# Moving weight conversions earlier and writing out the instruction order of 45 units by hand, in a kernel of attention and two MLP blocks

## The chip, the core and the metric

The kernel runs on one core of a Trainium2 chip. The metric is the device time of one execution in microseconds (us). The core has five engines that work side by side, each with its own queue in order: TensorE (PE in the profile, with its weight loads as PEld), VectorE (DVE), ScalarE (ACT), GpSimd (POOL), and SyncE (SP), which here issues nearly every DMA. An engine takes its instructions in the order in which the compiled program lists them; an instruction that waits holds up all that stand behind it on that engine.

## The reference

Inputs are float32. Batch is 4, sequence 576, width 512 (8 heads of 64).

```python
x = attention(q, k, v)                      # local band + pooled, (4, 576, 512)
xn = (x - mean) / sqrt(var + 1e-6) * g_ln
x = x + relu(xn @ w_ch1) @ w_ch2            # first MLP, hidden width 2048
h = relu(x.T @ w_tok1) @ w_tok2             # token mixing over the sequence, 576 -> 256 -> 576
u = x + h.T
out = u + relu(u @ w_ch1') @ w_ch2'         # second MLP, hidden width 1536
```

The weights arrive as float64 words (two int32 each), so the kernel must turn them into float32 on the chip and then split each into a high and a low float32r part; every product is three matmuls (high by high, high by low, low by high).

## The kernel before, in words

**Units.** The 2304 tokens are 18 tiles of 128, taken two at a time as 9 chunks of 256. A unit is one chunk against one block of 128 hidden columns: `g1` (12 matmuls, L883) into a PSUM bank of pool `h`, `relu` on ACT (L897), `low` on DVE (L901), then `g2` (6 matmuls, L916) into the chunk's accumulators `acc`. The first MLP has 16 blocks, so units 0 to 143 are chunks 0 to 8; the second has 12, so units 144 to 251 are chunks 9 to 17. `base[c]` is the first unit of chunk c: `base[7]` is 112, `base[8]` 128, `base[9]` 144, `base[10]` 156. From unit 157 on, units 1 to 10 of a chunk are done in pairs (`g1_pair` L994, `pair_sums`, `g2_pair` L1033) with fewer matmuls. A unit's program order is g1 of the next unit, its relu, its low, the steps of list `mid`, g2 of this unit, and the steps of list `bg`; the function `put(position, step)` files a step in the `mid` (whole number) or `bg` (half) list of a unit. A chunk's end (`evac` L925, `store`) writes the sums back.

**Weights.** A piece is half a block's weights, 128 x 512 values, 512 KB as it arrives. `convert_steps` makes float32 of it with three DVE instructions (L261, L266, L271) from a staging buffer `st` into a buffer `cv`, then splits it (ACT L276, DVE L279). For the second MLP the resident weight buffers come free only while chunk 8 runs, so 20 pieces (blocks 1 to 10) are converted ahead in `pre_f32` (L1331) and written by a DMA to a scratch tensor `w_scr` (L1339, 256 KB); `b_load` (L1341) reads a block back into `st` (L1347, 512 KB) and `b_split` (L1349) splits it (ACT L1358, DVE L1361). The four pieces of blocks 0 and 11 are never written out: they are loaded (L1325) and converted where they are split. There are three `st` buffers and, in this part, two `cv` buffers. `load_tok` (L1061) loads and converts the nine pieces of the token weights.

**Other steps around it.** A chunk's input is centred (`ln_center`), transposed in 32 x 32 blocks on DVE (`xt_t` L814), put in place by 4 groups of 4 DMAs for each of its 2 tiles (`xt_dma` L822), and split (`xp_hi` ACT L834, `xp_lo` DVE L839). Token mixing loads a tile (`xs_load` L1096), splits it on ACT (L1100) and POOL (L1101), and multiplies (`tok1` L1115, `tok2` L1150). `tq_load` and `tq_sums` (L977, L985, L986) make the combined weights for the pairs, from `w_scr`.

**Order.** Units 0 to 111 follow a table of steps written out by hand (`STEPS`), emitted under `manual_schedule`, which keeps the written order on every engine. What comes after is placed by a scheduler that works on a modelled timeline: it may put a step earlier than the program lists it, between the table's steps too. Only some instructions are held at their place in the program by `keep_in_program_order`: the first DVE instruction of each `pre_f32`, the first ACT instruction of each `b_split`, the first of each `ln_rstd` and of each `tq_sums`.

**Steps that the change and the prediction touch.** At `bt` = 112: `close_att` (L1300), all nine `load_tok`, and the first two `pre_load`. At units 113 to 132 (L1366): one `pre_f32` each. From unit 130 (`bw` = 128): `b_load` and, at half units from 131, `b_split` (L1369 to L1372). `put_prep1` (L1166) files a first-MLP chunk's preparation and `put_prep2` (L1181) that of a second-MLP chunk, with all eight groups of `xt_dma` directly behind the transposes; `put_tok` (L1174) files a batch's token mixing.

Of the kernel before, what the change touches and what calls it, by code (L numbers as in the profile page):

```python
# [9 lines left out]
I32 = mybir.dt.int32  # L10
# [34 lines left out]
FAST = 11  # L45
QF = DM // 2
# [22 lines left out]
    1; xt_lo 0 0; s_max 4; s_exp 4; ln_center 0 1; av_pe 3 1 acc; load 4 vw; raw 2 1; av_norm 3 1; s_pe 5 g; xt_pe 0
    1 acc; s_max 5; xt_hi 0 1; s_exp 5; load 5 vw; xt_lo 0 1; ex_pe 3 1 acc; t_pe 4 1 acc; x_add 3 1; c_a 4; load 6  # L70
    qk; ln_center 1 0; g1 0; ln_center 1 1; t_copy 4 1; td_pe 5 0 g; relu 0; c_b 4; t_pe 4 0 acc; td_copy 5 0; td_pe
    5 1 g; t_copy 4 0; raw 3 0; td_copy 5 1; xt_pe 1 0 acc; xt_hi 1 0; xt_lo 1 0; t_pe 5 1 g; avd_pe 5 g; load 6 vg;
    xt_pe 1 1 acc; t_copy 5 1; v_sums 4; xt_hi 1 1; avd_norm 5; low 0; t_pe 5 0 g; xt_lo 1 1; c_c 4; avd_pe 4 acc;
    t_copy 5 0; c_hi 4; c_lo 3; up_write 5; av_pe 4 g; av_z 4; g1 1; avd_norm 4; c_a 5; raw 3 1; av_act 4; relu 1;
    g1 2; c_lo 4; c_b 5; c_a 6; g2 0; low 1; av_pe 5 g; g2 1; g1 3; relu 2; c_c 5; av_z 5; low 2; g2 2; c_hi 5; c_b
    6; up_write 4; c_lo 5; c_c 6; av_act 5; up_read 5; c_a 7; relu 3; raw 4 0; low 3; load 6 vw; s_pe 6 g; c_hi 6;
    g1 4; g2 3; c_b 7; g1 5; c_lo 6; raw 4 1; c_c 7; c_hi 7; s_max 6; relu 4; s_exp 6; relu 5; loc_write 5; t_pe 6 0
    g; q_sums 6; c_a 8; c_lo 7; t_copy 6 0; low 4; c_b 8; c_a 9; c_c 8; g2 4; raw 5 0; d_pe 6 g; c_b 9; low 5; raw 5
    1; c_hi 8; c_c 9; c_hi 9; g1 6; raw 6 0; c_lo 8; d_max 6; g2 5; d_exp 6; c_a 10; c_lo 9; g1 7; load 7 qk; c_b
    10; relu 6; relu 7; td_pe 6 1 g; low 6; td_copy 6 1; c_c 10; c_a 11; low 7; td_pe 6 0 g; g2 6; v_sums 6; c_b 11;  # L80
    t_pe 6 1 g; raw 6 1; td_copy 6 0; c_hi 10; t_copy 6 1; avd_pe 6 g; c_lo 10; g2 7; c_c 11; c_a 12; avd_norm 6; g1
    8; g1 9; c_hi 11; relu 8; load 7 vg; c_b 12; c_lo 11; raw 7 0; c_c 12; c_a 13; low 8; q_sums 7; c_hi 12; av_pe 6
    g; c_b 13; c_lo 12; raw 7 1; g2 8; relu 9; c_c 13; low 9; c_hi 13; av_z 6; c_a 14; c_lo 13; g1 10; loc_read 5;
    av_act 6; c_b 14; relu 10; g2 9; c_a 15; g1 11; c_c 14; c_b 15; low 10; c_hi 14; c_c 15; s_pe 7 g; relu 11; c_hi
    15; raw 8 0; c_lo 14; s_max 7; c_a 16; s_exp 7; loc_write 4; low 11; c_b 16; g2 10; raw 8 1; g1 12; g2 11; c_lo
    15; c_c 16; relu 12; up_write 6; c_a 17; low 12; c_b 17; raw 9 0; raw 9 1; c_hi 16; d_pe 7 g; loc_write 6; g1
    13; d_max 7; c_lo 16; g2 12; g1 14; relu 13; c_c 17; d_exp 7; c_a 18; low 13; c_hi 17; relu 14; t_pe 7 0 g; c_b
    18; td_pe 7 1 g; t_copy 7 0; g2 13; c_lo 17; v_sums 7; raw 10 0; c_c 18; c_a 19; up_read 4; c_hi 18; low 14;
    loc_read 4; td_pe 7 0 g; g1 15; relu 15; g2 14; g1 16; av_add 5; raw 10 1; td_copy 7 1; c_b 19; c_lo 18; c_c 19;
    td_copy 7 0; low 15; raw 11 0; c_a 20; av_add 4; load 7 vw; c_hi 19; t_pe 7 1 g; c_b 20; c_lo 19; g2 15; c_c 20;  # L90
    g1 17; relu 16; c_hi 20; low 16; rstd; raw 11 1; relu 17; low 17; t_copy 7 1; g2 16; g1 18; relu 18; avd_pe 7 g;
    c_a 21; c_lo 20; c_b 21; g2 17; c_a 22; loc_read 6; g1 19; low 18; c_c 21; up_read 6; raw 12 0; g2 18; c_b 22;
# [12 lines left out]
    v_red 12 0; d_max 8; d_exp 8; v_mul 12 1; g2 31; relu 32; td_pe 8 1 g; td_copy 8 1; evac 29 1; v_red 12 1; td_pe
    8 0 g; evac 31 0; low 32; td_copy 8 0; load 9 qk; g1 33; v_mul 12 2; avd_pe 8 k; evac 29 0; relu 33; v_red 12 2;
    evac 31 1; av_pe 8 g; xt_dma 3 0 1; store 29 1; avd_norm 8; g1 34; v_mul 12 3; low 33; av_z 8; g2 32; v_red 12
    3; av_act 8; xt_dma 3 0 2; store 31 0; q_sums 9; s_pe 9 k; d_pe 9 g; store 29 0; v_mul 12 4; relu 34; rstd 2;
    v_red 12 4; g2 33; v_mul 12 5; load 9 vg; xt_dma 3 0 3; low 34; load 9 vw; xp_hi 3 0; s_max 9; loc_write 8; g1
    35; s_exp 9; load 10 qk; v_red 12 5; d_max 9; relu 35; g2 34; d_exp 9; g1 36; v_mul 12 6; xt_t 3 1; relu 36;  # L110
    t_pe 9 0 k; v_sums 9; v_red 12 6; t_copy 9 0; low 35; td_pe 9 0 k; s_pe 10 g; v_soft1 12; td_copy 9 0; up_write
    8; td_pe 9 1 k; t_pe 9 1 k; low 36; s_max 10; g2 35; v_sexp 12; td_copy 9 1; v_soft2 12; t_copy 9 1; avd_pe 9 k;
    g1 37; v_gm 12 0; store 31 1; avd_norm 9; s_exp 10; relu 37; q_sums 10; v_gm 12 1; loc_read 8; av_pe 9 g; low
    37; d_pe 10 k; xt_dma 3 1 0; g1 38; g2 36; g1 39; v_ga 12 1; v_load 13; up_read 8; av_z 9; av_add 8; xt_dma 3 1
# [85 lines left out]
def block_kernel(ctx: ExitStack, tc: tile.TileContext, qk, vw, vh, vg, g_ln, wa, t1, t2, wb, band, near, lv, edge, out):  # L200
# [46 lines left out]
    wt = {}  # L247

    wa, wb, t1, t2 = (w.bitcast(I32) for w in (wa, wb, t1, t2))

    def stage(n):
        return sp["pool"].tile([128, 2 * QW], I32, tag="st", name="st", bufs=sp["n"])[:, :2 * n]

# [57 lines left out]
    def split_unit(i, part, pinned=True):  # L311
        first, *rest = split_steps(i, part)
        ins = first()
        if pinned:
            tc.keep_in_program_order(ins)
# [1211 lines left out]
```

## Time and profile before

| | before |
|---|---|
| median of 3 runs | 886.04 us (884.27 to 886.44) |
| the profiled execution's own time | 888.04 us |
| its span, first to last instruction | 886.2 us |
| PE busy | 857.1 us (97%) |
| PEld busy | 775.9 us (88%) |
| DVE busy | 604.6 us (68%) |
| ACT busy | 302.0 us (34%) |
| POOL busy | 211.0 us (24%) |
| mean granted TensorE clock | 0.996 |

How to read it: busy time is the time in which at least one instruction of an engine is running. The profiled execution is one of its own; 1.84 us of it lie outside the span. A row's number after the start is its duration; a bracket at its end is the idle time just before it on its engine and what ended that. "SPq" rows are DMAs being issued, not their transfers.

### The profile page before, as it was taken

To read this page: it belongs to the slowest core of one execution; us is meant where nothing else is said; L and a number is where in the kernel's file an instruction comes from. 1 tells how busy PE (TensorE), PEld (TensorE's weight loads), DVE (VectorE), ACT (ScalarE), POOL (GpSimd) and SP (SyncE) were. 2 spreads that over 40 slices of the span, in tenths; PEclk is the share of its full clock that TensorE was granted. 3 is DMA by queue.
4 is the path that set the end of the run, shared out by engine and by line. 5 is a ranking of instruction groups with operands and counts; after the bars stand their busy time and mean duration, and the time that the engine had idled before them with its cause. 6 is when DMAs were issued, how large, how long until landed. Compare 5 with 4: busy or idle time off the path is not lost.

```text
span 886.2 us, 18074 instructions
## 1 busy us (share of the span) xinstructions
PE 857.1 (97%) x6778; PEld 775.9 (88%) x6778; DVE 604.6 (68%) x1345; ACT 302.0 (34%) x829; POOL 211.0 (24%) x213
## 2 busy tenths in 40 slices
PE   7989999999999999999997999999999999999997
PEld 6878899888889999888997887889999998999997
DVE  5999989998988776832376856665546545455454
ACT  5665535354321111312111134343333242323332
POOL 7731233467873510101000001001021011000000
PEclk9999999999999999999999999999999999999999
DMA  8646776467662522542187748322132122112100
GB/s 282 191 147 227 225 238 198 148 197 222 168 156 70 138 50 60 157 120 65 38 240 264 244 138 239 99 91 64 39 83 71 42 68 62 23 40 57 23 26 24
DMA packets 132518, 111.56 MB, mean 126 GB/s; under 512 B 79384, under 2 KB 105016, under 8 KB 132432
## 3 DMA queue, kind: packets, MB, share of 16 engines
q1 hardware_dynamic: 132432, 110.42, 43.5%
q8 instruction: 53, 0.87, 0.4%
q14 instruction: 33, 0.27, 0.1%
HBM read 80.73 MB, written 21.77 MB: 116 GB/s over the span
## 4 chain that ended last, share of the span: by engine, by line
PE 60%; DVE 17%; DMA 11%; SPq 6%; issue 3%; POOL 2%; ACT 1%; DVEq 0%; ACTq 0%; POOLq 0%
PE h L883 15%; PE acc L916 13%; PE h L994 11%; PE g L1033 6%; SPq L822 5%; PE acc L1033 4%; PE k L916 2%; DMA w_scr<-cv 2%; PE k L1115 2%; PE k L1150 2%; DMA et<-loc_scr 1%; DVE cv L266 1%; DMA st<-w_scr 1%; DVE ht L901 1%; DMA st<-in_wb_dram 1%
## 5 line engine op out<-in xcount | busy, mean ns | idle before, releaser
L883 PEld LDWEIGHTS h<-xt,w 128*128 128x128 f32 x2064 | 267.9, 191 | 19.0 <-DVE ht L901 5.6
L883 PE MATMUL h<-xt,w 128*128 128x256 f32 x2064 | 277.4, 284 | 5.6 <-DVE ht L901 5.0
L916 PE MATMUL acc<-w,ht 128*128 128x512 f32 x840 | 221.1, 398 | 4.5 <-DVE ht L901 3.9
L916 PEld LDWEIGHTS acc<-w,ht 128*128 128x128 f32 x840 | 150.0, 190 | 36.6 <-DVE ht L901 6.9
L897 ACT ACTIVATE ht<-h 128x256 fp32r<-128x256 f32 x156 | 60.0, 385 | 231.9 <-PE h L883 167.6
L994 PE MATMUL h<-xt,w 128*128 128x256 f32 x960 | 123.1, 283 | 0.0
L994 PEld LDWEIGHTS h<-xt,w 128*128 128x128 f32 x960 | 119.4, 191 | 2.7 <-issue 1.0
L901 DVE SCALAR_TENSOR_TENSOR ht<-h,ht 128x256 fp32r<-128x256 f32 x156 | 65.0, 417 | 63.8 <-ACT ht L897 63.0
L1101 POOL TENSOR_TENSOR xs<-xs 128x512 fp32r<-128x512 f32 x20 | 26.4, 1330 | 336.0 <-ACT xs L1100 229.2
L1011 DVE TENSOR_TENSOR hf<-hf 128x128 f32<-128x128 f32 x160 | 42.2, 304 | 65.3 <-ACT hf L1005 64.0
L1015 DVE TENSOR_TENSOR h<-hf,h 128x512 fp32r<-128x512 f32 x80 | 48.5, 643 | 22.8 <-ACT h L1014 22.7
L1014 ACT ACTIVATE h<-hf 128x512 fp32r<-128x512 f32 x80 | 42.1, 570 | 39.1 <-DVE hf L1011 39.1
L1005 ACT ACTIVATE hf<-h 128x256 f32<-128x256 f32 x80 | 26.3, 381 | 81.4 <-PE h L994 78.7
L688 POOL TENSOR_TENSOR lp<-lqk 128x576 f32<-128x576 f32 x28 | 40.0, 1428 | 42.7 <-DVE ls L694 30.6
L1048 POOL TENSOR_TENSOR x<-x,xc 128x512 f32<-128x512 f32 x8 | 11.3, 1413 | 159.8 <-ACT xc L1045 159.8
L659 POOL TENSOR_TENSOR x<-x,et 128x256 f32<-128x256 f32 (+2 forms) x40 | 33.0, 848 | 47.7 <-DMA et<-loc_scr 37.8
L271 DVE SCALAR_TENSOR_TENSOR cv<-st,cv 128x512 int32<-128x512 int32 (+4 forms) x63 | 43.1, 687 | 0.6
L839 DVE TENSOR_TENSOR xt<-xt 128x512 fp32r<-128x512 f32 x30 | 21.7, 724 | 31.6 <-ACT xt L834 30.4
L266 DVE SCALAR_TENSOR_TENSOR cv<-st,cv 128x512 int32<-128x512 int32 (+4 forms) x63 | 42.4, 675 | 0.6
L1033 PE MATMUL g<-w,h 128*128 128x256 f32 x240 | 40.7, 279 | 0.0
L261 DVE TENSOR_SCALAR cv<-st 128x512 int32<-128x512 int32 (+4 forms) x63 | 27.3, 434 | 16.1 <-DMA w_scr<-cv 10.5
L834 ACT ACTIVATE xt<-xt 128x512 fp32r<-128x512 f32 x30 | 18.9, 631 | 54.9 <-DMA xt<-xc 51.5
(245 smaller groups left out, 1234.1 us busy)
## 6 DMA issues: line engine op xcount, KB each, us to landing
st<-in_wa_dram SPq DMA_DIRECT2D x28, 512.0 KB
st<-in_wb_dram SPq DMA_DIRECT2D x24, 512.0 KB
xt<-xc SPq DMA_DIRECT2D x480, 16.0 KB
qk<-in_qk_dram SPq DMA_DIRECT2D x13, 581.0 KB
w_scr<-cv SPq DMA_DIRECT2D x20, 256.0 KB
st<-w_scr SPq DMA_DIRECT2D x10, 512.0 KB
x_scr<-x SPq DMA_DIRECT2D x18, 256.0 KB
x<-x_scr SPq DMA_DIRECT2D x9, 512.0 KB
```

What stands on the lines that cost most here:

```text
L266: nc.vector.scalar_tensor_tensor(out=f, in0=h, scalar=-0x40000000, in1=f, op0=ALU.bitwise_and, op1=ALU.bitwise_or)
L271: nc.vector.scalar_tensor_tensor(out=f, in0=l, scalar=29, in1=f, op0=ALU.logical_shift_right, op1=ALU.bitwise_or)
L822: nc.sync.dma_start(out=f32(xT[c])[32 * q:32 * q + 32, :, 1, n:n + 32], in_=xts[c, j][32 * i:32 * i + 32, :, q, :])
L883: nc.tensor.matmul(out=hp[:, :CN], lhsT=w[:, 0, a, kk * 128:(kk + 1) * 128], rhs=xT[c][:, kk, e, :], start=(n == 0), stop=(n == 3 * KD - 1),)
L897: nc.scalar.activation(out=t[:, 0], in_=hps[i][:, :CN], func=ACTF.Relu)
L901: nc.vector.scalar_tensor_tensor(out=t[:, 1], in0=hp[:, :CN], scalar=0.0, in1=f32(t[:, 0]), op0=ALU.max, op1=ALU.subtract)
L916: nc.tensor.matmul(out=acc[c, j], lhsT=t[:, a, j * 128:(j + 1) * 128], rhs=w[:, 1, e, :], start=(m == 0 and n == 0), stop=(last and n == 2),)
L994: nc.tensor.matmul(out=hp[:, k], lhsT=w[:, 0, a, kk * 128:(kk + 1) * 128], rhs=xT[c][:, kk, e, :], start=(n == 0), stop=(n == 3 * KD - 1),)
L1011: nc.vector.tensor_tensor(out=f[:, o], in0=f[:, x], in1=f[:, y], op=op)
L1014: nc.scalar.activation(out=hi, in_=v, func=ACTF.Copy)
L1015: nc.vector.tensor_tensor(out=lo, in0=v, in1=f32(hi), op=ALU.subtract)
L1033: nc.tensor.matmul(out=acc[c, k] if first else acc[c, k][:, o], lhsT=t[:, a, a_], rhs=tq["z"][k - 2] if first else w[:, e], start=first, s ...
```

## The change

The nine token pieces and the first seven of the pieces for scratch are converted by steps in the table; the other eleven follow in units 114 to 126. The steps are split: for scratch into load (`pl`), conversion (`pc`) and write (`pw`), for token pieces into load (`tl`), conversion with the high part (`tc`) and low part (`td`). There are three `cv` buffers instead of two. Six pieces are converted where they are split: both of block 0 and the first halves of blocks 1, 4, 7 and 11 (before, the four of blocks 0 and 11); the other 18 go through scratch (before, 20). Units 112 to 156 are emitted under `manual_schedule`; from unit 157 on, the scheduler places the steps as before. Transposes' DMAs are filed group by group, and token mixing of batches 0 and 1 is filed two units earlier.

The steps put into the table, each after the step named:

```
low 86:   close; tl 0; tl 1; tl 2        low 100:  td 8; pl 2; pc 0
low 90:   tc 0; tc 1                     low 103:  pw 0; pl 3; pc 1
low 91:   td 0; td 1; tl 3; tl 4; tc 2; tc 3
low 92:   td 2; td 3; tl 5; tl 6; tc 4   low 104:  pw 1; pl 4; pc 2
low 94:   td 4; tl 7; tc 5               low 105:  pw 2; pl 5; pc 3
low 95:   td 5; tl 8; tc 6               low 106:  pw 3; pl 6; pc 4
low 97:   td 6; pl 0; tc 7               low 107:  pw 4; pl 7; pc 5
low 99:   td 7; pl 1; tc 8               low 109:  pw 5; pl 8; pc 6
low 110:  rstd 7
```

```diff
+W1D = (1, 4, 7, 11)
...
     def put_prep1(c, e):
         for j in range(CT):
-            if c > 2:
-                put(e - 9.5 + j, ln_center, c, j)
-                put(e - 8.5 + j, xt_turn, c, j, None)
-                put(e - 3 + j, xt_part, c, j)
-        put(e + 4, ln_rstd, c)
+            put(e - 14.5 + 3 * j, ln_center, c, j)
+            put(e - 14 + 3 * j, lambda c=c, j=j: xt_t(c, j))
+            for i in range(4):
+                put(e - 13.5 + 4 * j + i, xt_dma, c, j, i)
+            put(e - 7.5 + 5 * j, xp_hi, c, j)
+            put(e - 7 + 5 * j, xp_lo, c, j)
+        put(e + 1.5, ln_rstd, c)
...
-            put(u + n, xs_load, b, n)
+            put(u + n if n > 1 else u + n - (1.5 if b else 3), xs_load, b, n)
...
-            put(e - 10 + 0.5 * j, lambda c=c, j=j: xt_turn(c, j, uch[c][:, j]))
-            put(e - 3 + j, xt_part, c, j)
+            put(e - 10 + 0.5 * j, lambda c=c, j=j: xt_t(c, j, uch[c][:, j]))
+            for i in range(4):
+                put(e - 9.5 + 3 * j + 0.75 * i, xt_dma, c, j, i)
+            put(e - 5 + 3 * j, xp_hi, c, j)
+            put(e - 4.5 + 3 * j, xp_lo, c, j)
...
+    pre = [(m, part) for m in range(1, UB) for part in range(NPC) if part or m not in W1D]
-    pre = [(m, part) for m in range(1, FAST) for part in range(NPC)]
...
-        sp["n"], sp["cv"] = 3, 2
+        sp["n"], sp["cv"] = 3, 3
...
-    put_tok(0, base[NCH - 1] - 4)
-    put_tok(1, base[NCH - 1] + 3)
+    put_tok(0, base[NCH - 1] - 6)
+    put_tok(1, base[NCH - 1] + 1)
+    def direct(m, part):
+        return m == 0 or part == 0 and m in W1D
     def b_load(m):
...
+            if direct(m, part):
+                b_raw(m, part)
+            elif direct(m, 0):
+                f = sp["pool"].tile([128, QW], I32, tag="cv", name="cv", bufs=sp["cv"])
+                ld_w["f", m, part] = f.bitcast(F32)
+                nc.sync.dma_start(out=f.bitcast(F32), in_=w_scr[m][:, part * QW:])
+            elif part == 0:
+                t = stage(QW).bitcast(F32)
+                nc.sync.dma_start(out=t, in_=w_scr[m])
...
-    for k in range(len(pre)):
-        put(bt + 1 + k, pre_load, k + 2)
-        put(bt + 1 + k, pre_f32, k)
-    put(bw + 2, b_load, 0)
+    for k, u in zip(range(7, len(pre)), (2, 3, 5, 6, 8, 9, 10, 11, 12, 13, 14)):
+        put(bt + u, pre_write, k - 1)
+        put(bt + u, pre_load, k + 2)
+        put(bt + u, pre_f32, k)
+    put(bt + 15, pre_write, len(pre) - 1)
     for m in range(UB):
-        put(bw + 3 + m, b_load, m + 1)
-        put(bw + 3.5 + m, b_split, m)
+        put(bw + 1 + m, b_load, m)
+        put(bw + 3 + m, b_split, m)
+        put(bw + 3.5 + m, b_lo, m, 0)
+        put(bw + 4 + m, b_lo, m, 1)
     for c in range(NCH, 2 * NCH):
-        put_prep2(c, base[c] - 1)
+        put_prep2(c, base[c] - (3 if c == NCH else 1))
...
+    with tc.manual_schedule():
+        walk(UNITS, 157)
+    man[0] = False
+    walk(157, NSEQ)
```

`b_split` now emits the conversion and the ACT high part, and `b_lo` the low part (and, for a direct piece, both parts of the split). `walk(lo, hi)` is the loop over units that stood at the end before.

## Rows read from the trace of the kernel before

**Rows 1.** The page's second part: busy tenths in 40 slices of 22 us.
```profile
PE   7989999999999999999997999999999999999997
```

**Rows 2.** Windows: length, busy time (count) of PE, PEld, DVE, ACT, POOL, clock, DMA share, GB/s.
```profile
400.00:433.00 33.00, 33.00 (x200) 28.19 (x199) 6.22 (x13) 6.41 (x15) 3.88 (x3) 1.00 0.15 43
433.40:485.60 52.20, 47.18 (x304) 42.72 (x302) 33.85 (x75) 7.58 (x19) 0.00 (x0) 0.98 0.72 226
485.60:589.70 104.10, 100.51 (x576) 86.64 (x577) 70.39 (x150) 34.44 (x76) 3.96 (x3) 0.98 0.56 168
480.00:485.00 5.00, 0.54 (x5) 0.34 (x3) 0.95 (x2) 0.38 (x1) 0.00 (x0) 0.83 0.59 217
485.00:490.00 5.00, 4.44 (x17) 4.06 (x18) 5.00 (x11) 0.00 (x0) 0.00 (x0) 0.50 0.61 172
```

**Rows 3.** PE's waits from 433 to 590: who waited for what, us in total, times, longest.
```profile
PE h L883 <- DVE ht L901: 5.0, 1, 5.0
PE acc L916 <- DVE ht L901: 1.8, 2, 1.4
PE k L1115 <- ACT xs L1100: 1.1, 1, 1.1
PE acc L916 <- ACT ht L897: 0.5, 1, 0.5
```

**Rows 4.** Timeline around the long wait: start, us, engine, line, operation.
```profile
478.94 0.69 DVE L271 SCALAR_TENSOR_TENSOR cv<-st,cv 128x512 int32<-128x512 int32 x1
...
480.58 0.38 ACT L897 ACTIVATE ht<-h 128x256 fp32r<-128x256 f32 x1 [2.43 <-PE h L883]
484.01 0.43 DVE L261 TENSOR_SCALAR cv<-st 128x512 int32<-128x512 int32 x1 [4.38 <-DMA w_scr<-cv]
...
485.08 0.42 DVE L901 SCALAR_TENSOR_TENSOR ht<-h,ht 128x256 fp32r<-128x256 f32 x1
```

**Rows 5.** The chain that ended last, in order of time: start, us, what.
```profile
425.54 1.43 PE h L883 x12
426.97 2.75 PE acc L916 x12
...
477.37 6.55 DMA w_scr<-cv
...
485.56 2.93 PE h L883 x12
488.49 3.56 PE acc L916 x12
...
532.22 6.39 DMA st<-w_scr
```

**Rows 6.** DVE's groups from 433 to 600: busy us, mean ns, idle before and releaser.
```profile
L271 DVE SCALAR_TENSOR_TENSOR cv<-st,cv 128x512 int32<-128x512 int32 x24 | 17.5, 733 | 0.4
L266 DVE SCALAR_TENSOR_TENSOR cv<-st,cv 128x512 int32<-128x512 int32 x24 | 16.3, 686 | 0.4
L1361 DVE TENSOR_TENSOR w<-st,w 128x512 fp32r<-128x512 f32 x20 | 13.2, 698 | 10.4 <-ACT w L1358 10.4
L261 DVE TENSOR_SCALAR cv<-st 128x512 int32<-128x512 int32 x24 | 10.1, 425 | 15.3 <-DMA w_scr<-cv 10.5 <-DMA st<-in_wb_dram 4.9
```

**Rows 7.** Timelines of SP, and of PE, POOL and DVE, in four places.
```profile
508.76 1.54 PE L1115 MATMUL k<-xs,t1w 128*128 128x512 f32 x6
...
516.15 13.63 SPq L822 DMA_DIRECT2D xt<-xc  x20
...
598.09 1.02 DVE L1011 TENSOR_TENSOR hf<-hf 128x128 f32<-128x128 f32 x4 [0.79 <-ACT hf L1005]
...
617.21 2.56 POOL L1101 TENSOR_TENSOR xs<-xs 128x512 fp32r<-128x512 f32 x2 [77.52 <-PE h L883]
617.71 2.61 DVE L1011 TENSOR_TENSOR hf<-hf 128x128 f32<-128x128 f32 x4 [0.73 <-ACT hf L1005]
...
620.90 0.50 PE L1033 MATMUL g<-tg,h 128*128 128x256 f32 x2 [1.44 <-ACT h L1014]
```

More of the change, by code (lines that the diff above doesn't have):

```diff
@@ L111 @@
[L111 to L114, printed above, removed]
-    1; v_gm 12 2; av_act 9; load 10 vg; xt_dma 3 1 2; d_max 10; v_ga 12 2; t_pe 10 1 g; v_gm 12 3; d_exp 10; relu
@@ new lines, in block_kernel @@
+    sp2_ctx = ExitStack()
+    steps = {f.__name__: f for f in (
+        q_sums, v_sums, s_max, s_exp, d_max, d_exp, t_pe, t_copy, td_pe, td_copy, avd_pe, avd_norm, ex_pe, x_add, expand,
+        up_write, up_read, loc_write, av_norm, av_act, load, fill, consts, band_in, masks, ln_center, xt_pe, xt_hi, xt_lo, g1,
+        relu, low, g2, evac, store, s_pe, d_pe, vec_open, v_load, v_loadv, v_mul, v_red, v_soft1, v_sexp, v_soft2, v_gm,
+        v_ga, v_store, loc_read, xt_t, xt_dma, xp_hi, xp_lo,
+    )}
@@ new lines, in block_kernel, with emit @@
+    steps.update(
+        close=close_att, tl=tok_load, tc=tok_conv, td=tok_lo, pl=pre_load, pc=pre_f32, pw=pre_write, av_pe=av_any, av_add=add_run, raw=load_unit, rstd=lambda c="first": ln_rstd(c, False), av_z=lambda n: av_norm(n, 0),
+        **{name: conv_step(k) for k, name in enumerate(("c_a", "c_b", "c_c", "c_hi", "c_lo"))},
+    )
+    def emit(table):
+        for step in table.split(";"):
+            name, *args = step.split()
+            steps[name](*(int(a) if a.isdigit() else a for a in args))
@@ new lines, in block_kernel @@
+    with tc.manual_schedule():
+        for z in rz:
+            nc.vector.memset(z, 1.0)
+        make_identity(nc, ident)
+        nc.vector.tensor_copy(identr, ident)
+        emit(STEPS)
+    rota[:] = ["g", "k"]
+    nl[0] = nsp[0] = len(pieces)
+    for c in range(8, NCH):
+        put_prep1(c, base[c] - 1)
+    bt = base[NCH - 2]
+    put(base[NCH - 1] - 5, rota.__setitem__, slice(None), ["g"])
+    put_tok(0, base[NCH - 1] - 6)
+    put_tok(1, base[NCH - 1] + 1)
+    def direct(m, part):
+        return m == 0 or part == 0 and m in W1D
@@ L1341, in b_load @@
     def b_load(m):
-        if m in (0, FAST):
-            for part in range(NPC):
+        t = None
+        for part in range(NPC):
+            if direct(m, part):
                 b_raw(m, part)
-        elif m < FAST:
-            t = ld_w["f", m] = stage(QW).bitcast(F32)
-            nc.sync.dma_start(out=t, in_=w_scr[m])
+            elif direct(m, 0):
+                f = sp["pool"].tile([128, QW], I32, tag="cv", name="cv", bufs=sp["cv"])
+                ld_w["f", m, part] = f.bitcast(F32)
[3 more added lines that the diff above has]
+                nc.sync.dma_start(out=t, in_=w_scr[m])
+            if t is not None:
+                ld_w["f", m, part] = t[:, part * QW:(part + 1) * QW]
```

390 lines of the change are left out of this document (198 added, 192 removed).

## The prediction

> **What bounds the kernel now.** The page's second part comes first: PE is busy in nearly every slice [rows 1]. Its 857.1 us of 886.2 leave 29.1 us idle, so only time in which PE idles or runs slowly can be won. Windows tell where. In 400 to 433, while the table's last units run, PE has no gap, while DVE is busy for 6.2 of 33 us [rows 2]. In 433.4 to 485.6 (units 112 to 127, where the pieces are converted for scratch) PE idles 52.20 - 47.18 = 5.0 us; in 485.6 to 589.7 (units 128 to 156, the blocks read back and split, token mixing) 104.10 - 100.51 = 3.6 us [rows 2]. PE's waits name the releasers: one wait of 5.0 us of a g1 for `low`, 1.8 us in two waits of g2 for `low`, 1.1 us for the ACT split of a token tile, 0.5 us for a relu [rows 3].
>
> The timeline shows how the 5.0 us arise [rows 4]. DVE ends a conversion at about 479.6; its next one, at 484.01, sat idle 4.38 us until a write `w_scr<-cv` had landed, since with two `cv` buffers piece k waits for the write of piece k-2. `low` stands behind it on DVE: its relu began at 480.58, it itself only at 485.08, and the PSUM bank that the next g1 needs is freed by it. The chain gives that write 6.55 us from issue to landing [rows 5]. The wait costs once more after it: the granted clock falls to 0.83 and 0.50 of full in the two windows of 5 us [rows 2], the lower level (1.2 GHz), and the next 12 g1 matmuls take 2.93 us and the 12 of g2 3.56 us, where the chain has 1.43 and 2.75 us before [rows 5]: 1.50 + 0.81 = 2.3 us.
>
> **The yardstick.** A unit is 1.43 + 1.38 = 2.81 us of PE. relu and low take 0.38 + 0.42 us [rows 4], some 0.9 us with the steps between, and their result is needed only after one g2 and one g1: `low` may be late by 2.81 - 0.9 = 1.9 us before PE stops. A token-mixing step of 6 matmuls adds about one g2, 1.4 us, judged by its like-shaped matmuls [rows 5, 7].
>
> **The change part by part.**
>
> *Earlier conversions.* One piece is 0.43 + 0.69 + 0.73 = 1.84 us of DVE [rows 6]. Seven move into units 100 to 109. With `low` at 0.42 that is 2.3 us in a unit of 2.8 us. Beside DVE's 6.2 us in 33 they fit, also with the token pieces, which merely spread over more units. Cost nothing; the cover is PE's own work, and if a load is late `low` has its 1.9 us. Left for units 114 to 126 are 11 pieces in 13 units, where 20 were to be done in 20 units with the transposes and splits between.
>
> *Third `cv` buffer and separate writes.* A write is issued in the step after its conversion, so SP no longer waits for DVE in front of it. Piece k now waits for the write of k-3, filed two units (5.6 us) before it. A write as slow as the worst row, 6.55 us, would be late by 0.9 us, less than the 1.9 us of slack. So the 5.0 us and the 2.3 us of slow clock go: 7.3 us. That is a size from one wait seen whole, and both ends are near: if a rest of the wait stays, it is below the limit and costs nothing, or it is above and a stall of this very size returns (a rival).
>
> *Loads one by one and spread transposes.* In 516 to 530 the queue of SP is taken by 20 transposing DMAs in 13.63 us, 0.68 us each [rows 7]; the reading of a block stood behind them and took 6.39 us more [rows 5]. ACT waits for the block, and a token split, relu and low behind it. The groups are now filed one at a time over seven units, so a load waits for one or two groups (2.7 or 5.5 us), not for eight. SP carries as many of these DMAs as before. Of the 3.6 us idle in 485.6 to 589.7 I take 2.5 us as won: the 1.1 us of the token split, and most of the 1.8 us for `low`. Ends: 0 and 3.6 us.
>
> *Six pieces direct.* Two more conversions, 2 x 1.84 = 3.7 us of DVE, now lie in units 131 to 142; two writes and the reading of as many halves go. DVE in units 131 to 134, in the written order: unit 131 has low 0.42, two conversions 3.7, two block transposes of some 0.7 and one addition of 0.7, 6.2 us; unit 132 has 0.4 + 1.84 + three low parts of 0.70, 4.3; unit 133 has 2.5; unit 134 has 1.8. Together 14.8 us, against 4 x 2.81 + 4 x 1.4 = 16.8 us of PE with token mixing. It fits, with the direct conversions hidden behind token matmuls. Bounds: 0 to 2.5 us lost, as worked out in the first rival. I take 0.5 us.
>
> *Program order for units 112 to 156.* SP, ACT, POOL and PE now take their steps as listed. PE: a token matmul is filed one unit behind its POOL split, whose ACT part is filed one unit behind its load where the `xs` buffers (two) hold the load back until the token matmul two before is done. A unit there has 4.2 us, so a tile has about 4 + 4 us from load to matmul. Nothing is lost as long as the load lands in some 4 us; behind it on ACT stands the next relu with 1.9 us of slack. SP: in units 113 to 120 eight groups of 2.7 us, 21.8 us, and five writes and loads of under 1 us each stand against 8 x 2.81 = 22.5 us. SP falls up to 3 us behind and catches up from unit 121, where no transposes are filed. Cost 0; if the cover goes, next late are the loads of pieces 13 and 14 and DVE with them.
>
> *From unit 157 on.* The scheduler places the steps as before, on another start. The row to go by is PE's idle 1.44 us before 620.90, while two POOL token splits run beside DVE [rows 7]. I take no change; ends are these 1.4 us won, or as many lost.
>
> **Sum.** 7.3 + 2.5 - 0.5 = 9.3 us. Against the profiled execution's own 888.04 us that is 878.7; the median of the runs stands 2.0 us lower, so 886.04 - 9.3 = **876.7 us**.
>
> **Rivals.**
>
> *1. DVE gives part of it back (about 881 us).* When two POOL splits ran beside four DVE additions, those took 2.61 us, where they take 1.02 us alone, and PE stopped for 1.44 us [rows 7]. So a POOL split can hold DVE up by about 0.8 us, or 1.6 us where two lie together. The window 485.6 to 589.7 holds three such splits [rows 2]; in the written order batch 1 has one each in units 130 to 134 beside the fullest DVE stretch, and batch 0 one each in units 123 to 127 beside conversions. Four times 0.8 to 1.6 us on 14.8 us makes 18.0 to 21.2, against 16.8 + 1.9 of slack: 0 to 2.5 us of PE, and 1 to 2 us of slow clock if it comes in one piece. Units 124 to 127 have 2.3 us of DVE in 4.2 and don't care. Price some 4 us. Against it: PE also has the second token step of unit 130 ahead of these units.
>
> The Trainium skill, SBUF — State Buffer, "Who interferes with whom", makes it a lock: a DVE instruction with two SBUF inputs and a GpSimd instruction that reads SBUF exclude each other for a whole instruction. By that rule two of a conversion's three instructions are held up; the row above agrees.
>
> *2. A new order that stalls (slower, about 890 us).* In program order ACT stands still if a block's read is late. From unit 136 a block is loaded two units ahead, 5.6 us, and relu adds 1.9: a read that needs over 7.5 us from its turn on SP to its landing stops PE. In units 133 to 136 six groups, 16.4 us of SP, are filed in 4 x 2.81 + 3 x 1.4 = 15.4 us, so the read for block 8 may start 3 to 4 us late and then need 6.4 us. One stall is priced by the old one, 5.0 + 2.3 = 7.3 us, which leaves 884; two of them, here and in units 113 to 121 or 144 to 150, give 876.7 + 14.6 = 891 us. Against it: the blocks behind are then loaded together, and the reading of the scratch stands in a quieter DMA stretch than the old write did.
>
> *3. Everything goes (874 us).* All 3.6 us and the 1.4 us after unit 157 are won, and nothing is given back: 886.04 - 7.3 - 3.6 - 1.4 = 873.7. For it: each of these waits has one late DMA or one crowded stretch of DVE behind it, and both are thinned out.
>
> *4. The wait only changes its place (886 us).* The written order may copy what the scheduler had done, with one stall like the old one elsewhere and small gains lost. Against it: of the 20 conversions of that stretch 11 stay.
>
> **How the numbers follow.** A measurement of this kernel can tell about 0.3% from no change, 2.7 us (883.4 to 888.7). Chances: the forecast, 874.5 to 879, 0.50; everything goes 0.15; partly given back, up to 883.4, 0.18; no change 0.08; slower 0.09. So faster 0.83, same 0.08, slower 0.09. The range for 8 in 10 runs from the third rival's end, 873.5, to one stall's 884.
>
> **What would show it.** Right: no DVE wait of over 2 us for `w_scr<-cv`, the granted clock at 1.00 from 433 to 590, PE idle there under 2 us, the first pair of chunk 10 some 9 us earlier, the same PE busy time less some 2 us. Rival 1: PE waits for `low` in units 131 to 137 with DVE without a gap. Rival 2: ACT waiting for `st<-w_scr` or `xt<-xc` with relu behind it and a window at clock 0.5. Wrong altogether: PE idle in units 86 to 111, where it now has none, or the time lost after unit 157, where the scheduler builds anew.

## The result and the profile after

The change makes the kernel slower: 891.4 us median of 17 runs (886.43 to 895.3) against 885.9 us (882.04 to 889.37) for the kernel before beside it, a ratio of 1.0065 with a 95% interval of 1.0048 to 1.0083. The forecast was 876.7 us. The profiled execution is the shortest of the 17, 886.43 us with a span of 884.7; a second profile of the same kernel (the first run below) has 891.81 and 890.1. Both are read here.

The waits of PE in 350 to 590 us, first profile:

```profile
PE acc L927 <- ACT ht L908: 6.0, 2, 3.6
PE acc L927 <- DVE ht L912: 3.9, 3, 2.6
PE k L1141 <- POOL xs L1127: 2.1, 3, 1.1
PE h L894 <- ACT xt L845: 0.7, 1, 0.7
```

The 5.0 us wait of [rows 3] is gone. In its place stand single waits of 2.4, 2.6 and 3.6 us, of g2 (L927, before L916) for a relu (L908, before L897) or a low (L912, before L901). The timeline tells what each is behind. Near 403, in the table:

```profile
396.98 2.52 SPq L833 DMA_DIRECT2D xt<-xc  x4
...
402.16 0.63 ACT L845 ACTIVATE xt<-xt 128x512 fp32r<-128x512 f32 x1 [6.66 <-DMA w_scr<-cv]
402.69 0.64 ACT L908 ACTIVATE ht<-h 128x256 fp32r<-128x256 f32 x2
...
403.11 1.98 PE L927 MATMUL acc<-w,ht 128*128 128x512 f32 x6 [2.42 <-ACT ht L908]
```

ACT stands idle for 6.66 us at the split of chunk 7's second tile (L845). The profile names a write, but what lands just before is the tile's last transposing group, issued at 396.98; two relus stand behind. Near 467 the waiting instruction is a conversion:

```profile
454.88 4.00 SPq L833 DMA_DIRECT2D xt<-xc  x4
...
458.93 0.59 SPq L1122 DMA_DIRECT2D xs<-x_scr  x1
459.62 0.37 SPq L1319 DMA_DIRECT2D w_scr<-cv  x1
...
460.04 0.43 SPq L1304 DMA_DIRECT2D st<-in_wb_dram  x1
...
464.63 0.83 DVE L272 TENSOR_SCALAR cv<-st 128x512 int32<-128x512 int32 x1 [6.50 <-DMA st<-in_wb_dram]
...
466.83 0.42 DVE L912 SCALAR_TENSOR_TENSOR ht<-h,ht 128x256 fp32r<-128x256 f32 x1
...
467.30 1.19 PE L927 MATMUL acc<-w,ht 128*128 128x512 f32 x4 [2.58 <-DVE ht L912]
```

The load of piece 13, filed in unit 120 behind the relu of unit 121, is issued at 460.04, 8.4 us after that relu began (451.64). From 433.51 until then SP had issued without a break: 28 transposing DMAs (20.0 us), four pairs of a write and a load at 1.1 us each, two token loads at 0.6. Near 537 the DMAs are those of chunk 9 and the reader is ACT, at block 8:

```profile
523.41 0.53 SPq L1304 DMA_DIRECT2D st<-in_wb_dram  x1
523.99 0.43 SPq L1381 DMA_DIRECT2D cv<-w_scr  x1
...
524.46 6.43 SPq L833 DMA_DIRECT2D xt<-xc  x8
...
530.99 1.48 SPq L1384 DMA_DIRECT2D st<-w_scr  x3
...
534.97 1.15 ACT L1401 ACTIVATE w<-st 128x512 fp32r<-128x512 f32 x2 [4.77 <-DMA st<-w_scr]
...
536.54 0.36 ACT L908 ACTIVATE ht<-h 128x256 fp32r<-128x256 f32 x1
...
536.96 0.73 PE L927 MATMUL acc<-w,ht 128*128 128x512 f32 x2 [3.63 <-ACT ht L908]
```

The reads of blocks 8, 9 and 10, filed in units 137 to 139, leave SP together at 530.99, behind eight transposing DMAs. The second profile stalls in the table and behind piece 13 again (3.0 and 2.6 us), but for only 0.8 us at block 8; near 517 a token tile is late instead (two waits, 2.0 us together). It shows what a stall costs behind it. Windows of 10 us (columns: stretch, its length, PE busy with its instructions, granted clock, DMA share, GB/s):

```profile
400.00:410.00 10.00, 6.99 (x38) 0.90 0.66 193
410.00:420.00 10.00, 10.00 (x65) 0.93 0.84 277
470.00:480.00 10.00, 7.42 (x33) 0.83 0.94 326
510.00:520.00 10.00, 7.89 (x34) 0.87 0.63 184
```

All but the second, which follows the first, have 2.1 to 3.0 us of idle PE in them, and the granted clock falls to the lower level (1.2 GHz) for part of the stretch or of the next one. In the first profile only the longest stall is followed by this (0.92 and 0.91 in 530 to 550). The mean clock of the 17 runs is 0.997 in the shortest and 0.989 to 0.996 in the others. Between the two profiles PE's idle time is the same (30.4 and 29.7 us, where before had 29.1), and PE's busy time is 6.1 us longer in the second (860.4 against 854.3): 3.3 us of it ahead of unit 87, where nothing was changed (a window at 0.83 in 60 to 70 us), the other 2.8 us behind it, most of it at the stalls shown. So the first profile is a lucky one. Most of the loss against the kernel before is slow clock and not idle time: from the relu of unit 87 on, the two profiles have 18.7 and 17.3 us of idle PE where before has 16.4, while the mean clock is 0.992 over the 17 runs and 0.996 to 0.997 over the runs of the kernel before that stand beside the experiments. A share of 0.004 to 0.005 of 890 us is about 4 us, of 5.5 us lost (an estimate).

### The profile page after: what moved, and what is told of

Its sections match the earlier page's. It is cut to its first block, busy times and chain, and to the rows that moved or that the text cites. A ratio compares the mean times of both kernels' runs of the same rounds, so it can differ in the third digit from the quotient of the medians.

```text
span 884.7 us, 18065 instructions
## 1 busy us (share of the span) xinstructions
PE 854.3 (97%) x6778; PEld 774.4 (88%) x6778; DVE 607.7 (69%) x1345; ACT 302.2 (34%) x829; POOL 209.3 (24%) x213
## 4 chain that ended last, share of the span: by engine, by line
PE 68%; DVE 14%; SPq 6%; DMA 6%; issue 2%; ACT 2%; POOL 1%; DVEq 0%; ACTq 0%; POOLq 0%
PE h L894 18%; PE acc L927 15%; PE h L1005 13%; PE g L1044 7%; SPq L833 5%; PE acc L1044 5%; PE k L1176 3%; PE k L927 2%; PE k L1141 2%; DVE cv L277 1%; DVE cv L282 1%; DVE ht L912 1%; DMA qk<-in_qk_dram 1%; DMA st<-in_wb_dram 1%; DMA xt<-xc 1%
## 5 line engine op out<-in xcount | busy, mean ns | idle before, releaser
L927 PE MATMUL acc<-w,ht 128*128 128x512 f32 x840 | 218.8, 397 | 11.2 <-ACT ht L908 6.0
L927 PEld LDWEIGHTS acc<-w,ht 128*128 128x128 f32 x840 | 149.7, 189 | 42.4 <-DVE ht L912 7.9
L908 ACT ACTIVATE ht<-h 128x256 fp32r<-128x256 f32 x156 | 60.0, 385 | 234.6 <-PE h L894 188.3
L912 DVE SCALAR_TENSOR_TENSOR ht<-h,ht 128x256 fp32r<-128x256 f32 x156 | 65.1, 417 | 62.9 <-ACT ht L908 62.5
L1026 DVE TENSOR_TENSOR h<-hf,h 128x512 fp32r<-128x512 f32 x80 | 46.5, 619 | 17.9 <-ACT h L1025 17.8
L1059 POOL TENSOR_TENSOR x<-x,xc 128x512 f32<-128x512 f32 x8 | 10.8, 1356 | 165.7 <-ACT xc L1056 165.7
L1044 PE MATMUL acc<-w,h 128*128 128x256 f32 x240 | 36.4, 280 | 0.0
L1044 PEld LDWEIGHTS g<-w,h 128*128 128x128 f32 x240 | 34.0, 188 | 0.6 <-issue 0.5
```

The lines of the kernel that those rows point to most:

```text
L908: nc.scalar.activation(out=t[:, 0], in_=hps[i][:, :CN], func=ACTF.Relu)
L912: nc.vector.scalar_tensor_tensor(out=t[:, 1], in0=hp[:, :CN], scalar=0.0, in1=f32(t[:, 0]), op0=ALU.max, op1=ALU.subtract)
L927: nc.tensor.matmul(out=acc[c, j], lhsT=t[:, a, j * 128:(j + 1) * 128], rhs=w[:, 1, e, :], start=(m == 0 and n == 0), stop=(last and n == 2),)
L1026: nc.vector.tensor_tensor(out=lo, in0=v, in1=f32(hi), op=ALU.subtract)
L1044: nc.tensor.matmul(out=acc[c, k] if first else acc[c, k][:, o], lhsT=t[:, a, a_], rhs=tq["z"][k - 2] if first else w[:, e], start=first, s ...
```

## The experiments

**Theory S**: in program order SP, the only queue for DMAs, runs late behind the transposing DMAs; ACT or DVE then stands at a tile, block or piece that has not landed, the next relu or low stands behind it, PE stops, and its clock falls. **Rival R**: the conversions, moved and made direct, crowd DVE whatever the DMAs do. **Rival L** is the prediction's first: POOL splits hold DVE up. The first expectations also name O (the written order costs everywhere, by many short waits at full clock) and T (the table's new steps are the cause).

The table gives all of them (ratio to the kernel before, run beside each; PE idle is the length of a stretch less PE's busy time in it, in the profiled execution: from the relu of unit 87 to that of 113, from there to that of 155, and from there to the end).

| kernel | median us | ratio, 95% interval | idle 87-112 | idle 113-154 | idle from 155 |
|---|---|---|---|---|---|
| before | 885.9 | 1 | 0.6 | 8.5 | 7.2 |
| after | 891.4 | 1.0065 (1.0048 to 1.0083) | 3.7 | 9.4 | 5.6 |
| after_again | 891.8, one run | | 4.1 | 5.9 | 7.3 |
| one_copy | 875.4 | 0.9888 (0.9847 to 0.9930) | 0.7 | 1.5 | 6.8 |
| sched_112 | 881.2 | 0.9943 (0.9920 to 0.9967) | 5.8 | 0.3 | 5.8 |
| before_cv3 | 882.6 | 0.9959 (0.9935 to 0.9984) | 1.3 | 5.1 | 7.2 |
| table_late | 886.5 | 1.0003 (0.9983 to 1.0023) | 0.8 | 8.5 | 5.8 |
| groups_spread | 885.1 | 0.9997 (0.9975 to 1.0020) | 4.4 | 2.7 | 6.2 |
| spread_late | 879.9 | 0.9938 (0.9915 to 0.9961) | 1.1 | 3.8 | 6.4 |
| sched_late | 877.8 | 0.9921 (0.9897 to 0.9945) | 6.6 | 0.0 | 5.2 |
| spread_9 | 882.6 | 0.9956 (0.9930 to 0.9982) | 1.5 | 4.2 | 7.2 |
| all_scratch | 884.7 | 0.9990 (0.9959 to 1.0020) | 0.9 | 6.7 | 5.8 |
| scratch_cv2 | 885.9 | 1.0001 (0.9975 to 1.0027) | 1.1 | 7.3 | 6.4 |
| spread_dve | 883.3 | 0.9967 (0.9939 to 0.9994) | 1.9 | 4.2 | 5.6 |
| early_dve | 877.4 | 0.9913 (0.9879 to 0.9947) | 1.3 | 2.9 | 5.6 |
| early_pool | 882.0 | 0.9961 (0.9937 to 0.9985) | 0.8 | 4.4 | 5.6 |

Medians of different rows stand beside different runs of the kernel before (885.2 to 886.8), so rows are compared by their ratios.

**after_again**: the changed kernel as it is.

> The changed kernel itself, in one more profiled execution, since the first one profiled (886.4 us) is the fastest of 17 and 5 us below their median. Theory S (SP's queue: loads stand behind transposing DMAs, and the written order turns a late load into a late relu or low): the same places stall as in the first profile, longer, with windows at a granted clock near 0.5; span some 889 to 891 us. Theory O (the written order costs everywhere, by token splits and DVE): the extra time is spread over many waits under 1 us, clock 0.99 or more everywhere.

891.81 us. Two of the three stalls are there again and the third is shorter, as shown above, and the clock falls behind them: S, and not O.

**sched_112**: units 112 to 156 go back to the scheduler, all else as after.

```
-    with tc.manual_schedule():
-        walk(UNITS, 157)
     man[0] = False
+    walk(UNITS, 157)
     walk(157, NSEQ)
```

> The changed kernel with units 112 to 156 left to the scheduler; table, pieces and buffers as changed. If the written order of those units is the cause (S and O alike): 879 to 885 us, the stalls near 467 and 537 gone, that near 403 kept. If the table's new steps are the cause (theory T): 889 to 892 us, as the changed kernel.

881.19 us: the written order alone costs 1.2% (1.0065 against 0.9943), and without it PE idles 0.3 us in units 113 to 154. The same conversions, direct pieces and buffers now gain. In the table PE idles more than in after (5.8 us), and mostly for another reason: 4.7 us of it are four waits for low, the longest 1.6, and 1.2 us one wait for a relu.

**one_copy**: for the tiles of chunks 7, 8 and 9, one plain DMA replaces the 16 transposing ones; the exchange of 32 x 32 blocks between partitions is left out.

```
     def xt_dma(c, j, i):
...
+        if c in (7, 8, 9):
+            if i == 0:
+                n = slice(j * 128, (j + 1) * 128)
+                nc.sync.dma_start(out=f32(xT[c])[:, :, 1, n], in_=xts[c, j].rearrange("p k q n -> p k (q n)"))
+            return
```

> The changed kernel with one DMA in place of the sixteen that put a transposed tile in place, for chunks 7, 8 and 9; it leaves out the exchange of blocks between partitions there. S: with SP's queue short, the stalls near 403, 467 and 537 go, and the time falls to 875 to 881 us. O: it stays at 888 us or above. T: the stall near 403 goes only if SP is its cause; otherwise 3 us stay.

875.35 us, with the order of after kept. Taking SP's transposing DMAs away removes the stalls in the table and behind it together: 2.2 us idle in units 87 to 154 where after has 13.1. The conversions are all still there, so rival R falls. This edit changes the transfers as well as the queue; the runs with spread groups below keep every DMA and part the two.

**before_cv3**: the kernel before, with three `cv` buffers and nothing else.

```
-        sp["n"], sp["cv"] = 3, 2
+        sp["n"], sp["cv"] = 3, 3
```

> The kernel before with a third buffer for converted pieces and nothing else. If the 5.0 us wait of before and its slow clock hang on the two buffers: 877 to 880 us, no DVE wait over 2 us for the write to scratch. If the writes are limited by the DMA engines as such, the wait only moves: 884 to 887 us.

882.64 us, 3.6 us under the kernel before. The long wait goes, shorter waits come or stay:

```profile
PE acc L916 <- ACT ht L897: 2.7, 2, 1.4
PE h L883 <- DVE ht L901: 1.2, 1, 1.2
PE acc L916 <- DVE ht L901: 0.7, 2, 0.4
```

These are PE's waits of this kernel in 437 to 584 us. The buffer alone is thus worth half of the 7.3 us that the prediction gave for it and the separate writes.

The next four part the places. **table_late** moves only the ACT and DVE part of chunk 7's second tile in the table, which no g1 needs before unit 112; **groups_spread** only the positions of the DMAs of chunks 8 and 9; **spread_late** has both; **sched_late** has the table's edit, with the scheduler for units 112 to 156.

```
table_late:
-g2 100; relu 102; low 101; xp_hi 7 1; low 102; xp_lo 7 1; g2 101;
+g2 100; relu 102; low 101; low 102; g2 101;
-relu 106; low 106; pw 3;
+relu 106; xp_hi 7 1; low 106; xp_lo 7 1; pw 3;
groups_spread, put_prep1 and put_prep2:
-                put(e - 13.5 + 4 * j + i, xt_dma, c, j, i)
-            put(e - 7.5 + 5 * j, xp_hi, c, j)
-            put(e - 7 + 5 * j, xp_lo, c, j)
+                put(e - 13.5 + 1.5 * (4 * j + i), xt_dma, c, j, i)
+            put(e - 6.5 + 5.5 * j, xp_hi, c, j)
+            put(e - 6 + 5.5 * j, xp_lo, c, j)
-                put(e - 9.5 + 3 * j + 0.75 * i, xt_dma, c, j, i)
-            put(e - 5 + 3 * j, xp_hi, c, j)
-            put(e - 4.5 + 3 * j, xp_lo, c, j)
+                put(e - 9.5 + (4 * j + i if c == NCH else 3 * j + 0.75 * i), xt_dma, c, j, i)
+            put(e - 5 + (4.5 if c == NCH else 3) * j, xp_hi, c, j)
+            put(e - 4.5 + (4.5 if c == NCH else 3) * j, xp_lo, c, j)
```

> As after, but in the table the ACT and DVE part of chunk 7's second tile stand behind relu 106 and low 106 instead of behind relu 102. Theory S (in program order an engine stands at a tile whose transposing DMAs are late, with the next relu behind it): the PE waits of 2.4 to 3.0 us near 403 and the slow clock behind them go, PE idles under 1.6 us in units 86 to 111, and the time is 3 to 5 us under that of after, 886.5 to 888.5. Theory R (the earlier conversions themselves crowd DVE in the table): the idle time stays 3.5 us or more, and the time stays at 891.

> As after, program order for units 112 to 156 kept; only the positions of the transposing DMAs of chunks 8 and 9 change: one group in 1.5 units for chunk 8 (units 113 to 124, before 113 to 120), one in each unit for chunk 9 (131 to 138, before 131 to 136), and the ACT and DVE parts of their tiles later by 0.5 to 1.5 units. Theory S: the reads of pieces and of block 8 are issued in time, the waits near 467 (2.6 us for low behind a conversion) and 537 (3.6 us for relu behind the split of block 8) go, PE idles under 4 us in units 112 to 154, 881 to 885 us in all. Theory R (DVE is too full there with conversions beside POOL splits, whatever the DMAs do): the waits for low stay, 888 to 891.

> Both edits of the two runs before. Theory S: the gains add, PE idles under 5 us in units 86 to 154, no window after 200 us has a clock under 0.95, and the time comes near that of the run with one plain DMA per tile (875.4): 876 to 880 us. Theory R: 886 to 891.

> Units 112 to 156 left to the scheduler, and the table's edit for chunk 7. Theory S: of the 5.8 us of idle PE in units 86 to 111 of the run without the table's edit, the 1.2 us for a relu and the 0.7 us for low behind it go; the three waits for low behind conversions that the scheduler packs (3.9 us) stay: 878.5 to 880.5 us. If the whole 5.8 us came from the tile, 875.

886.48, 885.09, 879.93 and 877.77 us: all four speak for S and against R, though only spread_late lies inside the range of S (table_late and groups_spread are 0.1 us or less outside, sched_late 0.7 us below). The profiled execution of spread_late is the slowest of its seven (883.72 us) and has a window at 0.84 of the clock in 480 to 490, which S had excluded. The two edits add: 0.0062 in the ratio for the table's, 0.0068 for the spreading, 0.0127 for both, 11.2 us of 886. Two steps moved by four units in the table were thus worth 5 us. In spread_late the reads of blocks go out one by one between the groups, and block 8, read at 526.66 behind one group, holds ACT up for 0.60 us:

```profile
524.04 2.52 SPq L833 DMA_DIRECT2D xt<-xc  x4
...
526.66 0.53 SPq L1384 DMA_DIRECT2D st<-w_scr  x1
...
527.24 2.52 SPq L833 DMA_DIRECT2D xt<-xc  x4
...
529.85 1.25 SPq L1384 DMA_DIRECT2D st<-w_scr  x1
...
530.84 1.16 ACT L1401 ACTIVATE w<-st 128x512 fp32r<-128x512 f32 x2 [0.60 <-DMA st<-w_scr]
```

For a later block ACT still waits up to 1.95 us, and PE does not. In sched_late the 6.2 us of waits for low in the table (three, the longest 2.7) remain, more than the 3.9 expected: the scheduler moves conversions in front of `low` there. Its gain over sched_112, 0.0022, is within the intervals, so the 5 us of the table's edit are shown only for the order written by hand.

**spread_9**: table_late with chunk 9's part of groups_spread alone.

> As table_late (886.5 us), with chunk 9's transposing groups alone spread (one in each unit, 131 to 138). It parts the 6.5 us that the spreading of both chunks gave between the read of block 8 (relu waits 3.2 us near 537, with a slow clock behind it) and the loads of the pieces (low waits 2.6 us near 467). By the waits and the slow windows of table_late the stall at block 8 costs 3.2 us and some 0.5 to 1.5 us of clock: 881.5 to 883 us. If the two stalls had one cause, in chunk 8's groups alone, it stays at 886.

882.63 us, inside what was expected. The stall near 537 is gone, and the 2.6 us for low near 467 stands, with a clock of 0.92 and 0.91 in 460 to 480 behind it. Of the spreading, 0.0047 (4.2 us) is chunk 9's groups: the read of block 8, and whatever else stands behind them on SP, as the token tile near 517 in the second profile of after. The rest to spread_late, 0.0018, is within the intervals.

**all_scratch** gives up the direct halves (all of blocks 1 to 11 through the scratch); **scratch_cv2** is that with two `cv` buffers.

```
all_scratch, from spread_late:
-W1D = (1, 4, 7, 11)
+W1D = ()
-    for k, u in zip(range(7, len(pre)), (2, 3, 5, 6, 8, 9, 10, 11, 12, 13, 14)):
+    for k, u in zip(range(7, len(pre)), range(2, 17)):
-    put(bt + 15, pre_write, len(pre) - 1)
+    put(bt + 17, pre_write, len(pre) - 1)
scratch_cv2, from all_scratch:
-        sp["n"], sp["cv"] = 3, 3
+        sp["n"], sp["cv"] = 3, 2
```

> As spread_late, without the direct pieces in the blocks 1, 4, 7 and 11: 22 instead of 18 pieces go through the scratch, and their conversions fill units 114 to 128, one in each. The prediction priced the direct pieces at 0.5 us lost, against 0 to 2.5. If four conversions more in units 114 to 128 fit as those did, 878 to 881 us; if DVE or SP is full there, PE waits for low behind a conversion in units 118 to 128, 882 to 886 us, and the direct pieces are then a gain.

> As all_scratch, with two cv buffers instead of three: conversion k waits again for the write of piece k-2 to land. The prediction gave the third buffer and the separate writes 7.3 us together; in the kernel before, the third buffer alone gave 3.6 us. If that wait is the cause: a PE wait for low behind a conversion that waits for its write, of 1 to 3 us each, and 3 to 7 us more than all_scratch. If the write lands in time with the transposing DMAs spread: within 1 us of all_scratch.

884.67 and 885.9 us. Without the direct pieces the kernel is some 4.6 us slower than spread_late (0.9990 against 0.9938, with intervals that just touch), and a token matmul waits 3.2 us for its ACT split near 472. That more DMAs and conversions before unit 128 make the token tiles late is a reading of that wait and was not tested by itself. The third buffer is worth 1 us here, less than the intervals can tell; the long wait of [rows 4] does not return with two: DVE waits for a write for 2.65 us at most, PE for low for 0.9.

**spread_dve**, **early_dve** and **early_pool** look at the POOL splits. The first has the low part of the token tiles of batches 0 and 1 on DVE; the second also has chunk 8's groups every 1.25 units; the third has these groups and POOL.

```
spread_dve, from spread_late:
-        nc.gpsimd.tensor_tensor(out=t[:, 1], ...
+        (nc.vector if b < 2 else nc.gpsimd).tensor_tensor(out=t[:, 1], ...
early_dve, from spread_dve; early_pool, from spread_late:
-                put(e - 13.5 + 1.5 * (4 * j + i), xt_dma, c, j, i)
-            put(e - 6.5 + 5.5 * j, xp_hi, c, j)
-            put(e - 6 + 5.5 * j, xp_lo, c, j)
+                put(e - 13.5 + 1.25 * (4 * j + i), xt_dma, c, j, i)
+            put(e - 7.5 + 5 * j, xp_hi, c, j)
+            put(e - 7 + 5 * j, xp_lo, c, j)
```

> As spread_late (879.9 us), with the subtraction that makes the low part of the token tiles of batches 0 and 1 (units 123 to 134) on DVE instead of POOL, ten instructions. In spread_late one of these POOL splits (1.65 us) ran beside a subtraction of DVE for xt that took 1.75 us where it takes 0.69 us alone, and PE waited 1.9 us for it. Theory L (a POOL split holds up DVE beside it): that wait shrinks under 1 us, the waits of token matmuls for POOL (0.8 us) go, 877 to 879 us. Rival F (DVE is full there, and seven us more of work on it delay low): PE waits for low of over 1 us come in units 123 to 134, 880 to 884 us.

> As spread_dve, with chunk 8's transposing groups every 1.25 units instead of 1.5 (units 113 to 122) and their ACT and DVE parts back at units 119 to 125, where after has them. If SP keeps up, the PE wait for the turned tile of chunk 8 (1.9 us) is gone and nothing comes in its place: 876 to 878 us. If SP is late again, the wait for low near unit 122 returns with 1 to 2.6 us, 879 to 882.

> As early_dve (877.4 us), with the token tiles' low part on POOL again: chunk 8's groups every 1.25 units are the only difference from spread_late (879.9). Theory S (the 2 to 3 us between those two came from the turned tile of chunk 8 that landed late): 876.5 to 878.5 us, PE waits for POOL of about 1 us stay. Rival 1 of the prediction (POOL splits that hold DVE up are what is left): 879.5 to 881 us.

883.26, 877.39 and 881.96 us. spread_dve lies in the range of its rival F, but its longest wait is another one: PE waits 2.5 us for the turned tile of chunk 8, although the subtraction for it takes 0.68 us now.

```profile
472.45 0.62 ACT L845 ACTIVATE xt<-xt 128x512 fp32r<-128x512 f32 x1
...
477.16 0.69 DVE L282 SCALAR_TENSOR_TENSOR cv<-st,cv 128x512 int32<-128x512 int32 x1
477.77 0.68 DVE L850 TENSOR_TENSOR xt<-xt 128x512 fp32r<-128x512 f32 x1
478.51 1.58 PE L894 MATMUL h<-xt,w 128*128 128x256 f32 x11 [2.54 <-DVE xt L850]
```

The tile had landed and its ACT part was done at 473.07; the subtraction began 4.7 us later, behind two conversions, a low and a token subtraction that stand ahead of it in the order. So that wait came from the place of the step, not from POOL and not from a late transfer. early_dve, which files both parts of the tile earlier, is without it. It has the lowest ratio of the versions that compute all, 0.9% under the kernel before, but is not told apart from sched_late or spread_late. early_pool is above both of its ranges: the wait for the tile is gone, but token matmuls wait 2.2 us for ACT splits and 1.9 us for POOL splits, and the clock falls to 0.83 in 470 to 480. By the medians neither edit helps alone and both together do; the interval of spread_late overlaps all three, so this is not shown. Between early_pool and early_dve, where POOL or DVE is the only difference, 0.0048 (4 us) stand, with intervals that overlap slightly. The lengthening of DVE's instructions itself is plain. In the second profile of after:

```profile
483.02 1.74 POOL L1127 TENSOR_TENSOR xs<-xs 128x512 fp32r<-128x512 f32 x1 [2.07 <-ACT xs L1126]
483.65 1.67 DVE L282 SCALAR_TENSOR_TENSOR cv<-st,cv 128x512 int32<-128x512 int32 x1
```

and the same DVE instruction of early_dve, with no POOL split beside it:

```profile
473.73 0.69 DVE L282 SCALAR_TENSOR_TENSOR cv<-st,cv 128x512 int32<-128x512 int32 x1
```

By the Trainium skill, SBUF — State Buffer, "Who interferes with whom", a DVE instruction with two SBUF inputs and a GpSimd instruction that reads SBUF lock each other out of a shared port for a whole instruction. The rows agree: 0.69 us and 1.29 us alone (the POOL split at 461.14 in the first profile of after), 1.67 and 1.74 us together.

## Why the prediction was wrong

**The step that failed is "Program order for units 112 to 156", costed at 0.** By sched_112 it cost 0.0122 in the ratio, some 10.8 us of the 14.7 us between the forecast and the result. The prediction held that nothing is lost as long as a load lands in some 4 us, that SP falls up to 3 us behind, and that next late would be the loads of pieces 13 and 14 and DVE with them. The last is exactly what happened, but SP was 8.4 us late at piece 13 and not 3. The sum had "five writes and loads of under 1 us each" in units 113 to 120; a piece there is a write and a load, 1.1 us together, and two token loads of batch 0 fall into the same units. From 433.51 to 460.04 SP issued for 26.5 us, while PE took 19.7 us from the relu of unit 114 (431.90) to that of unit 121. Between a load's turn and its conversion lie two units of 2.8 us, 5.6 us, less than the 8.4.

**Its second rival is what happened.** It named block 8, whose read would start 3 to 4 us late and need 6.4 us against 7.5 us of slack. It started about 8 us late (530.99, against 522.69 for the relu of unit 138), and needed 4.0. It stalled PE for 3.6 us in the first profile and 0.8 in the second, and the spreading that removes it gives 4.2 us, where 7.3 was the price of a stall. That the rival's 891 us came about all the same is in part luck: three smaller stalls did it instead of two, one of them in the table. What was wrong was its chance, 0.09. Its own arithmetic (9.4 to 10.4 us needed, 7.5 there) said that it would stall; against it stood only that the blocks behind load together, which helps none of those that wait for the first.

**"Earlier conversions", cost nothing with PE's work as cover**: wrong in the table, by 5 us with the clock (table_late). DVE did fit, but for one wait of 1.1 us. But the token matmuls that the scheduler had moved into this stretch were gone (24 between the relus of units 87 and 101 before, none after), so PE came to unit 101 some 5 us earlier (relu to relu, 41.3 us behind unit 87 instead of 46.3), while the transposing DMAs of chunk 7's second tile were issued as late as before, 48.6 us behind unit 87 instead of 48.8. The split of that tile stood at its old place in the order, and ACT waited there for 6.66 us, where the kernel before has 0.64:

```profile
390.63 11.03 SPq L822 DMA_DIRECT2D xt<-xc  x16
...
402.99 0.63 ACT L834 ACTIVATE xt<-xt 128x512 fp32r<-128x512 f32 x1 [0.64 <-DMA xt<-xc]
```

The prediction's "wrong altogether", PE idle in units 86 to 111, was this.

**"Third `cv` buffer and separate writes", 7.3 us**: the wait goes, as said; the buffer alone measured 3.6 us in the kernel before. With the DMAs spread and all pieces through the scratch, a third buffer is worth nothing that can be told.

**"Loads one by one and spread transposes", 2.5 us won**: lost instead, since at 0.75 units a group chunk 9's DMAs were filed faster than SP issues them. Filed one in a unit, they do what this step promised.

**"Six pieces direct", 0.5 us lost**: by all_scratch a gain of some 4.6 us, with intervals that just touch. **Rival 1** (POOL beside DVE) is real in the durations; its share of the time stays open, from nothing (spread_dve) to 4 us (early_dve against early_pool). **"From unit 157 on", no change**: right within what the profiles tell, 5.6 and 7.3 us of idle time from unit 155 on against 7.2; the wait of 1.44 us before 620.90 [rows 7] has no counterpart in either profile of after.

With the DMAs out of the way the kernel takes 875.4 us, with the order mended 877.4 or 877.8, where 876.7 was forecast. That is near by luck and not by the forecast's terms: the third buffer, part of 7.3 us there, gave 3.6 us in the kernel before and about 1 us in the changed one, and the direct pieces gave some 4.6 us instead of costing 0.5.

## What to carry to other kernels

When an order is fixed by hand, cost the queue that issues DMAs like an engine: add up its issues, small ones too, against the time of the units that they are filed in, and take a queue that is over its time as a stall and not as a risk. In program order an instruction that waits for a DMA belongs as late as its reader allows, since everything behind it on its engine waits with it. And when work moves away from a stretch, ask which late transfer it had covered there.

## What the runs showed that was not expected

A transposing DMA of 16 KB keeps SP for 0.63 us (2.52 us for four, at times up to 4.00), more than the load of a piece of 512 KB (0.33 to 0.53 us). What fills the queue here is the number of its DMAs, not their bytes. Idle PE of 2 to 4 us was followed by windows of 10 us at 0.79 to 0.96 of the clock in most profiles, at times not (the first profile of after, near 403 and 467; sched_late, with a wait of 2.7 us), so that one and the same order differs by some 3 us between two profiles. The Trainium skill, DMA: Bandwidth & Descriptors, "Issuing engines are not separate DMA queues", says that issuing from several engines saves only the issue time, which it calls usually small beside the DMA itself. Here it was the bound, by the rows above; whether a second issuing engine would have helped, no run here shows.
